# A fused layer-norm kernel: the third row tile loaded alone between Wq and Wk, four roots on ScalarE, and the first transposes in two PSUM banks

## The chip, the cores and the metric

The kernel runs on one core of one Trainium2 chip. The metric is the device time of one execution in microseconds; the span in a profile (first to last instruction) is some 1.7 us shorter than the time of the same run. In the text PE is TensorE, DVE is VectorE, ACT is ScalarE, POOL is GpSimd and SPq is the queue of loads that SyncE issues; PSUM is the memory that PE's results land in, and Wq, Wk and Wv are the thirds of Wqkv.

## The reference, cut to what matters

```python
xn = _layernorm(x)                                  # x: 1 x 2048 x 512, bfloat16
return x + _A_ref(xn, A_wqkv, A_wo) + _B_ref(xn, B_w_gate, B_w_up, B_w_down)
# _A_ref: q, k, v = xn @ wqkv; 32 heads; each row attends to 8 rows, two apart; then @ wo
# _B_ref: (gelu(xn @ w_gate) * (xn @ w_up)) @ w_down
```

Nothing can be multiplied before the first 128 rows of x are loaded, normalised and transposed.

## The kernel before

The kernel is a graph of tasks. A list scheduler in the file orders them by simulated times and priorities when the kernel is built; on the chip each engine runs its list in order and waits on semaphores (in r6 below a copy whose data were there at 7.6 us runs at 9.39, behind the root ahead of it). x is cut into 16 row tiles of 128 rows, four tiles to a block. The first block is handled tile by tile: statistics, mean and root, subtraction, reciprocal, scaling, four transposes on PE, a copy out of PSUM on ACT, then the Q and K projections of that tile.

```python
for i, nm in enumerate(("q", "k", "v")):            # loads of Wqkv, by columns
    ...
    t_w = G.task("sp", "ld_w" + nm, 0, mk(), wr=[(I_wq, nm)],
                 prio=(-958, -957.5, -898)[i], nbytes=512 * 1024)
# ...
if p == 0:                                          # tiles 0 and 1: two loads, ahead of Wq
    ...
else:                                               # tiles 2 and 3: one load, behind Wk (prio -957)
    t_x = G.task("sp", "ld_x%d" % p, 0, mk_ld(), wr=[(it_x, 0), (it_x, 1)], prio=..., nbytes=256 * 1024)
# ...
if t < NSQA:                                        # NSQA = 2: the roots of tiles 0 and 1
    t_of["sq%d" % t] = G.task("act", "sq%d" % t, 0.15, mk_sa(), ..., table="sqrt")
else:                                               # other tiles: add eps on DVE, power 0.5 on GpSimd
    t_of["ve%d" % t] = G.task("dve", "ve%d" % t, 0.09, mk_ve(), ...)
# ...
chain(["bnst0", "bnag0", "sub0", "rstd0", "norm0", "bnst1", "bnag1", "sub1", "rstd1", "norm1",
       "bnst2", "bnag2", "ve2", "sub2", "bnst3", "rstd2", "norm2", "bnag3", "ve3", "sub3", "rstd3",
       "norm3", "bnst4"])                           # DVE's order
# ...
chain(warm_tasks[:WARM[0]] + ["tpx0_0"] + warm_tasks[WARM[0]:] +
      ["mmt0_0", "tpx0_1", "mmt1_0", "mmt0_1", "tpx1_0", "mmt1_1", "tpx1_1",
       "mmt0_2", "mmt1_2", "mmt0_3", "mmt1_3"])     # PE's order; mmt0_t is Q of tile t, mmt1_t is K
```

`SHIFT` is a table of priority offsets by group of tasks, found by search. It decides the order of everything that follows the start.

## Time and profile before

| | before |
|---|---|
| time, median of three runs | 197.85 us (197.62 to 197.93) |
| span of the profiled run | 196.0 us |
| PE busy | 190.6 us, 97% |
| transposes of tile 3 start | 12.15 us |
| last matmul ends | 193.55 us |

The views are read in the prediction below. From the transposes of tile 3 on, PE works without a pause to its last matmul. I call the time from the start of these transposes to that end "the train"; before, it is 193.55-12.15 = 181.40 us. Behind it lies a tail of 2.4 us, the last addition and store.

### The profile page before, as it was taken

Reading aid. Unit: us, or ns where it says so; the run is one execution under the profiler, and the core shown is the slowest. Engines: PE = TensorE matmul, PEld = TensorE weight load, DVE = VectorE, ACT = ScalarE, POOL = GpSimd, SP = SyncE. Lnnn points to the kernel's source line nnn. Section 1 sums busy time; section 2 is a strip of 40 time slices with the busy share of each in tenths; the row PEclk is TensorE's granted clock in tenths of the full one; section 3 lists DMA queues with packets and bytes.
Section 4 is the critical chain, followed back from the end, with each engine's and each line's share of the span. In section 5 each row is a group of like instructions: output and inputs, shape, how many; then the busy total and the mean of one; then the engine's idle time right before and its main releaser. Section 6 shows DMA issues by size and latency. Waiting matters only on the chain.

```text
span 196.0 us, 3243 instructions
## 1 busy us (share of the span) xinstructions
PE 190.6 (97%) x1223; PEld 91.1 (46%) x1223; DVE 153.8 (79%) x241; ACT 104.0 (53%) x169; POOL 9.6 (5%) x33
## 2 busy tenths in 40 slices
PE   7879999999999999999999999999999999999995
PEld 2675444444444344444444444443444444344484
DVE  5689997999699899989989984999966638962232
ACT  3467674777976649502647801667739500776000
POOL 6021000101000000000001100000000000000000
PEclk9999999999999999999999999999999999999999
DMA  5999998949934452262399346003892250020121
GB/s 137 364 410 274 331 201 138 270 116 229 213 72 108 107 151 68 64 168 93 107 204 222 61 113 183 27 0 110 211 229 43 57 160 29 27 59 0 33 87 40
DMA packets 34783, 27.03 MB, mean 138 GB/s; under 512 B 11248, under 2 KB 33232, under 8 KB 34768
## 3 DMA queue, kind: packets, MB, share of 16 engines
q1 hardware_dynamic: 34768, 26.83, 54.0%
q8 instruction: 9, 0.15, 0.3%
q14 instruction: 6, 0.05, 0.1%
HBM read 19.99 MB, written 5.26 MB: 129 GB/s over the span
## 4 chain that ended last, share of the span: by engine, by line
PE 93%; DMA 3%; DVE 2%; SPq 1%; issue 0%; POOL 0%; DVEq 0%
PE PS L1357 36%; PE PS L1436 19%; PE PS L1120 18%; PE PS L1432 7%; PE PS L1326 4%; PE PS L1204 4%; DMA XIN<-in_A_x_dram 3%; PE PS L1076 2%; PE PS L1392 2%; PE PS L1197 1%; DVE st L945 1%; SPq L881 0%; SPq L929 0%; DVE XIN L1001 0%; POOL sq L969 0%
## 5 line engine op out<-in xcount | busy, mean ns | idle before, releaser
L1436 PE MATMUL PS<-Wd,HT 128*128 128x512 bf16 (+2 forms) x209 | 41.3, 345 | 0.0
L1357 PE MATMUL PS<-xnT,Wu 128*128 128x512 bf16 x160 | 40.6, 379 | 0.0
L1357 PE MATMUL PS<-xnT,Wg 128*128 128x512 bf16 x160 | 40.3, 379 | 0.0
L1367 ACT ACTIVATE GG<-PS 128x512 bf16<-128x512 f32 x40 | 23.7, 601 | 28.9 <-PE PS L1357 27.7
L1305 DVE TENSOR_TENSOR UNI<-BS,PT 128x2048 bf16<-128x2048 bf16 x32 | 37.1, 1217 | 2.2 <-PE PS L1326 0.8
L1174 DVE TENSOR_TENSOR UNI<-QT,KT 128x2048 bf16<-128x2048 bf16 x32 | 37.4, 1217 | 0.3 <-PE PS L1326 0.3
L1120 PE MATMUL PS<-xnT,Wqkv 128*128 128x512 bf16 x160 | 36.0, 379 | 0.0
L1374 ACT ACTIVATE UU<-PS 128x512 bf16<-128x512 f32 x40 | 24.0, 600 | 10.5 <-PE PS L1357 10.4
L1436 PEld LDWEIGHTS PS<-Wd,HT 128*128 128x128 bf16 x209 | 19.6, 98 | 18.6
L1456 DVE TENSOR_TENSOR OB<-PS,XR 128x512 bf16<-128x512 f32 (+2 forms) x19 | 11.5, 605 | 17.7 <-PE PS L1436 17.7
L1357 PEld LDWEIGHTS PS<-xnT,Wg 128*128 128x128 bf16 x160 | 15.2, 98 | 19.8 <-issue 0.8
L1357 PEld LDWEIGHTS PS<-xnT,Wu 128*128 128x128 bf16 x160 | 15.4, 98 | 19.4 <-ACT GG L1367 0.8
L1120 PEld LDWEIGHTS PS<-xnT,Wqkv 128*128 128x128 bf16 x160 | 15.4, 98 | 19.2 <-ACT KT L1137 0.4
L1379 DVE TENSOR_TENSOR HT<-GG,UU 128x512 bf16<-128x512 bf16 x40 | 16.1, 420 | 8.8 <-ACT UU L1374 8.4
L1144 ACT ACTIVATE VT<-PS 128x512 bf16<-128x512 f32 x16 | 9.6, 598 | 14.4 <-PE PS L1120 14.4
L1432 PE MATMUL PS<-Wo,OT 128*128 128x512 bf16 (+2 forms) x76 | 16.9, 345 | 0.0
L945 DVE BATCH_NORM_STATS2 st<-XIN 128x6 f32<-128x512 bf16 x16 | 10.6, 684 | 2.0 <-DMA XIN<-in_A_x_dram 2.0
L1337 ACT ACTIVATE OT<-PS 128x512 bf16<-128x512 f32 x16 | 8.7, 594 | 5.4 <-PE PS L1326 5.4
L1432 PEld LDWEIGHTS PS<-Wo,OT 128*128 128x128 bf16 x76 | 7.2, 98 | 7.0
L1137 ACT ACTIVATE KT<-PS 128x512 bf16<-128x512 f32 x12 | 7.2, 597 | 4.8 <-PE PS L1120 4.8
L1130 ACT ACTIVATE QT<-PS 128x512 bf16<-128x512 f32 x12 | 7.2, 598 | 3.8 <-PE PS L1120 3.8
L969 POOL TENSOR_TENSOR sq<-ve,mhalf 128x2 bf16<-128x2 f32 (+1 forms) x8 | 5.5, 686 | 64.3 <-DVE ve L956 64.3
(62 smaller groups left out, 134.1 us busy)
## 6 DMA issues: line engine op xcount, KB each, us to landing
BS<-vt_scratch SPq DMA_DIRECT2D x64, 128.5 KB, 3.5
vt_scratch<-VT SPq DMA_DIRECT2D x16, 128.0 KB
XR<-in_A_x_dram SPq DMA_DIRECT2D x16, 128.0 KB, 2.1
XIN<-in_A_x_dram SPq DMA_DIRECT2D x7, 256.0 KB, 5.9
out_dram<-OB SPq DMA_DIRECT2D x14, 128.0 KB, 2.0
Wqkv<-in_A_wqkv_dram SPq DMA_DIRECT2D x3, 512.0 KB, 4.3
Wg<-in_B_w_gate_dram SPq DMA_DIRECT2D x1, 1280.0 KB
Wu<-in_B_w_up_dram SPq DMA_DIRECT2D x1, 1280.0 KB
```

What stands on the lines that cost most here:

```text
L945: return lambda e: e.bn_stats(out=st[:, t, :], in_=XIN[:, it.slot, t2, :])
L1120: ins = e.matmul(PS[:, 512 * it.slot:512 * it.slot + HWD], lhsT=lhsT, rhs=xnT[:, itx.slot, kt, c0:c0 + HWD], start=(kt == 0), stop=(kt == 3))
L1144: return lambda e: e.activation(out=VT[:, ito.slot, 0:HWD], in_=PS[:, 512 * it.slot:512 * it.slot + HWD], func=ACTF.Identity)
L1174: return lambda e: e.tensor_tensor(out=UNI[:, it.slot, :, :], in0=bass.AP(QT, (itq.slot * 4 + g) * 512, [[NQT * 4 * 512, 128], [0, 4], [1, ...
L1305: return lambda e: e.tensor_tensor(out=bass.AP(UNI, ito.slot * 2048, [[NUNI * 2048, 128], [512, 4], [128, 4], [1, 128]]), in0=bass.AP(BS, ...
L1357: ins = e.matmul(PS[0:M, 512 * it.slot:512 * it.slot + 512], lhsT=Wx[:, kt, j * 128:j * 128 + M], rhs=xnT[:, itx.slot, kt, :], start=(kt = ...
L1367: return lambda e: e.activation(out=GG[0:M, ito.slot, :], in_=PS[0:M, 512 * it.slot:512 * it.slot + 512], func=ACTF.Gelu_apprx_tanh)
L1374: return lambda e: e.activation(out=UU[0:M, ito.slot, :], in_=PS[0:M, 512 * it.slot:512 * it.slot + 512], func=ACTF.Identity)
L1379: return lambda e: e.tensor_tensor(out=HT[0:M, ito.slot, j, :], in0=GG[0:M, ig.slot, :], in1=UU[0:M, iu.slot, :], op=ALU.mult)
L1432: ins = e.matmul(PS[:, 512 * it.slot:512 * it.slot + CW], lhsT=OT[:, ito.slot, dq, ti * 128:(ti + 1) * 128], rhs=Wo[:, dq, c0:c1], start=( ...
L1436: ins = e.matmul(PS[:, 512 * it.slot:512 * it.slot + CW], lhsT=HT[:, ith.slot, j, ti * 128:(ti + 1) * 128], rhs=Wd[:, j, c0:c1], start=Fal ...
L1456: return lambda e: e.tensor_tensor(out=OB[:, ito.slot, 0:CW], in0=PS[:, 512 * it.slot:512 * it.slot + CW], in1=XR[:, itx.slot, c0:c1], op= ...
```

## The change

Its intent: have tile 2 on the chip before DVE is free for it, shorten DVE's work on tiles 2 and 3, and begin the first projection sooner. All priority shifts were searched anew as well.

```diff
 SHIFT = {
-    "acc0": 47, "acc1": -436, "acc3": 127, ...
+    "acc0": 361, "acc1": -284, "acc3": -893, ...        # every value is new
-    NSQA = cfg.get("NSQA", 2)
+    NSQA = cfg.get("NSQA", 4)                            # roots of tiles 0 to 3 on ScalarE
-        WARM = cfg.get("WARM", (9, 1))                   # 9 + 1 warm-up matmuls of 512 columns
+        WARM = cfg.get("WARM", ([512] * 8 + [128], [512, 128]))
...
-            if p == 0:
+            if p < 2:                                    # four loads of one tile each
                 for t2 in range(2):
...
-                    t_x = G.task("sp", "ld_x0_%d" % t2, 0, mk_ld(), wr=[(it_x, t2)], prio=-960 + t2,
+                    t_x = G.task("sp", "ld_x%d_%d" % (p, t2), 0, mk_ld(), wr=[(it_x, t2)],
+                                 prio=((-960, -959), (-957.8, -956.5))[p][t2], nbytes=128 * 1024)
...
+                it_t2 = Item("tpy" + nm, P_ps, "tp") if nm == "0_0" else it_tp      # a second bank
-                                c0 = 1024 * it.slot + kt * 128 * n + q * 128
+                                c0 = 1024 * (it, it2)[kt // 2].slot + kt * 128 * n + q * 128
...
+                if p == 0 and grp[0] == 0:               # DVE copies half of tile 0 out
+                    t_of["evy" + nm] = G.task("dve", "evy" + nm, d_dve(256), mk_ev2(), rd=[it_t2], ...)
...
+        chain(["bnst0", "bnag0", "sub0", "rstd0", "norm0", "bnst1", "bnag1", "evy0_0", "sub1", "rstd1", "norm1",
+               "bnst2", "bnag2", "sub2", "rstd2", "norm2", "bnst3", "bnag3", "sub3", "rstd3", "norm3", "bnst4"])
+                chain(["evk0_0", "sq3"])
```

The queue's order becomes tile 0, tile 1, Wq, tile 2, Wk, tile 3, Wv. Dead code (two tiny touch loads that were never issued) goes as well.

## The prediction

Some passages are cut: figures and rules that no trace or run shows. In the numbered list the second item speaks of ACT and the last of PE's matmuls. The sum came to 197.85-1.35 = 196.5 and, with 0.1 taken off the gain, 196.6. One step loses its ground, the time of ACT's half of the first copy, on which tile 1's root at 6.25 rests. An estimate from the trace of before can stand for it: one column on ACT takes 0.20 us (L850) and 512 take 0.60 (L1037), so 256 take some 0.40, from 5.54 to 5.94, and the root behind them 0.29 (L959), to 6.23. The first projection at 6.1 stands on DVE's half (5.92 to 6.05), which is the later one. "The gate opens" means here that the step between matmuls of 128 columns falls, from 0.107 us in the first transposes to 0.056 in the first projection.

> **What bounds the kernel now.** I read the page first (busy shares, then the slices), then the chain that ended last, then the timeline of the first 16 us, then the waits of the DMA queue. The page says that TensorE is the bound:
>
> ```profile
> PE 190.6 (97%) x1223; PEld 91.1 (46%) x1223; DVE 153.8 (79%) x241; ACT 104.0 (53%) x169; POOL 9.6 (5%) x33
> ...
> PE   7879999999999999999999999999999999999995
> ```
>
> The only slices of PE below nine tenths are the first four and the last one. The chain (start us, length us, what) says what those first slices wait for:
>
> ```profile
> 2.74 5.37 DMA XIN<-in_A_x_dram
> ...
> 8.13 0.70 DVE st L945
> ...
> 10.19 0.35 DVE XIN L1001
> ...
> 10.90 0.61 POOL sq L969
> ...
> 11.74 0.36 DVE XIN L1001
> ...
> 12.15 0.40 PE PS L1026 x4
> 12.55 3.57 PE PS L1076 x64
> ```
>
> After 12.15 every piece of the chain is PE and each begins where the last one ended, up to 193.56; then the last addition and store take the span to 196.0. So the end is 12.15 plus a fixed train of matmuls plus the tail. What moves the time is when that train can begin. Before 12.15 the chain is the third and fourth row tiles: one load that lands at 8.11, the statistics of tile 2 and tile 3 on DVE, and tile 3's root on POOL. The PE timeline shows the hole:
>
> ```profile
> 5.06 0.63 PE L1026 MATMUL PS<-ident,XIN 128*128 128x128 bf16 x4
> 5.49 0.63 PE L864 MATMUL PS<-wsrc 128*128 128x512 bf16 x1
> 6.39 1.07 PE L1076 MATMUL PS<-xnT,Wqkv 128*128 128x128 bf16 x16 [0.26 <-ACT xnT L1037]
> 7.29 0.39 PE L1026 MATMUL PS<-ident,XIN 128*128 128x128 bf16 x4
> 7.51 1.95 PE L1076 MATMUL PS<-xnT,Wqkv 128*128 128x128 bf16 x32
> 10.61 0.40 PE L1026 MATMUL PS<-ident,XIN 128*128 128x128 bf16 x4 [1.14 <-DVE XIN L1001]
> ```
>
> L1026 is a tile's transposes, L1076 its Q or K projection (16 matmuls, 0.90 us apart start to start: 7.29-6.39), L864 the warm-up. PE has nothing real between 9.46 and 10.61, because tile 2 isn't normalised. Two smaller things: the ninth warm-up matmul holds the first transposes to 5.06 though their weight load began at 4.84, and the copy-out of 0.60 us (5.73, ACT L1037) delays the first projection to 6.39. The queue's own waits give the arrival of Wk:
>
> ```profile
> SPq L890 <- DMA Wqkv<-in_A_wqkv_dram: 1.5, 1, 1.5
> ```
>
> L890 loads Wg and is made to wait for Wk; it issues at 7.46, so Wk had landed at 7.44. The projection that needs Wk starts at 7.51: Wk is just in time today.
>
> [...]
> 1. [...]adding up the GB/s slices of the first 12 us, the two first tiles (262 KB) are through near 3.0 us, Wq (786 KB) near 5.2, Wk (1311 KB) near 6.6, the 256 KB load (1573 KB) near 7.3; Wk is known to have landed at 7.44 and the load at 8.11, both some 0.8 us later than their last bytes. [...]
> 2. [...]0.60 us for 512 columns [...], 0.29 to 0.30 for the root with its eps pointer; one table load at 0.79, the next at 19.36, so two more roots near 8 and 10 us cause none.
> [...]
> 4. [...]the warm-ups are 0.43 apart, the first transposes 0.11, the first projection 0.056. So the gate opened between 5.5 and 6.4 us.
>
> **The change part by part.**
> *Warm-up, first copy.* Eight warm-ups and one of 128 columns end at 1.25 + 8 x 0.427 + 0.107 = 4.77 instead of 5.09, so the transposes go when norm 0 allows, near 4.87 (5.06 before): -0.19. Their data is there at 5.69-0.19 = 5.50. [...] DVE copies the other 256, but must first end its aggregate (5.60): from 5.63. This trace's f32 read of 256 PSUM columns on DVE takes 0.42 and of 128 takes 0.29, so I estimate 0.29 to 0.42: ends 5.92 to 6.05. Projection 0 starts near 6.1 instead of 6.39: -0.3.
> *Tile 1.* The DVE copy delays its subtraction from 5.64 to about 6.0, ending 6.35 to 6.4. But the root on ACT, which follows the copy there, comes at 6.25 instead of 6.52. So reciprocal 6.42 to 6.58, scaling to about 6.95 (7.10 before). A wash, slightly early.
> *Tile 2's load.* It moves ahead of Wk: 786 + 131 = 917 KB, whose bytes are through near 5.55; plus the lag of 0.8 it lands near 6.4, against 8.11. DVE is only free at 6.95, so the DMA wait of 1.04 us before L945 goes, and DVE decides. Wk's price is 131 KB at 0.38 KB/ns, 0.35 us: it lands near 7.8. Tile 3's half ends the same bytes as before: about 8.1.
> *Tiles 2 and 3 on DVE.* Before, tile 2 took from 8.13 to 10.54, 2.41 us, with the ve step (0.15), POOL (0.61) and tile 3's statistics in its way. With its root on ACT, tile 0 took from 2.94 to 4.79: 1.85 us. So tile 2: 7.0 to 8.85 (its root on ACT at 7.9 to 8.3, behind the copy of tile 1, which costs me 0.1). Tile 3: 8.95 to 10.8, against 12.09.
> *PE.* Projection q0 6.1 to 7.0, transposes of tile 1 7.03 to 7.25, then a new wait for Wk to 7.8; k0 to 8.7, q1 to 9.6, transposes of tile 2 (ready since 8.9) to 9.82, k1 to 10.72, transposes of tile 3 at about 10.8. Both chains, DVE's and PE's behind Wk, meet within 0.1 us. The unbroken train starts at 10.8 instead of 12.15: -1.35.
> *After that.* Wv follows at 2097 KB, about 9.6, and is wanted at 15.96-1.35 = 14.6; Wg, which waits for Wk, is late by 0.35 at most, and its bytes are through near 13.5, wanted at 18.55-1.35 = 17.2. Neither binds. The matmul work and the last stores are the same; the new shifts only reorder it, and there is no idle PE left there to win.
> Sum: 197.85 - 1.35 = 196.5. I take 0.1 off the gain for small losses in the reordered train: 196.6.
>
> **The rivals.**
> *Wk becomes the wait and eats it.* For: it is just in time today and goes behind 131 KB, and its order on PE is fixed. Against: PE loses at 7.25 to 7.8, where it had over a microsecond of hole later. If Wk came at 8.3, the train would start at 11.3: 197.0.
> *ACT's queue.* ACT gets two roots but also evictions of 0.60 us each, in order. If an eviction of q or k goes ahead of the root of tile 2 or of tile 3, each costs up to 0.6 on DVE's chain: train at 11.3 to 11.5, 197.0 to 197.2. For: ACT is nearly full from 7.7 to 9.3 in the timeline. Against: the roots have the higher priority, and tile 3's is explicitly placed behind k0's eviction, as if this had been looked at.
> *The reordered train has holes.* All shifts are new, so a wait of some tenths for DVE, which is 79% busy and nearly full from 12 to 47 us, or for a PSUM bank may appear: 196.8 to 197.9. Against: the earlier order has none, and everything upstream comes earlier.
> *A cold clock.* If the gate opens as late as 6.4 while q0 starts at 6.1, 0.15 us is lost, all of it inside the wait for Wk: nothing.
>
> **Range and chances.** PE idles only 196.0-190.6 = 5.4 us in all, of which 1.25 is the start before any operand exists and 2.4 the tail. Faster by 2% would be 3.96 us, which needs the train at 8.2, before tile 3 has even been normalised in any version: 1%. Slower by 2% needs 5.3 us of new holes: 1%. Within 2%: 98%. The range: a gain of 1.85 if the DVE chain runs without a hitch and Wk comes early (196.0), a gain of 0.55 if ACT or a hole takes its share (197.3).
>
> **What would show it.** Right: the load of tile 2 lands before 7 us and L945 no longer waits for a DMA there; no POOL root before 12 us; transposes of tile 3 near 10.8; a PE wait of about half a microsecond for Wk, Wg's issue near 7.8; PE without idle time from there to the end; projection q0 near 6.1. Wrong: tile 3's transposes after 11.5 (then ACT's order or Wk), or PE idle time after 12 us (then the shifts), or a tail other than 2.4 us.

## The result and the profile after

| | before | after |
|---|---|---|
| time, median of four runs each | 197.88 us (197.62 to 197.93) | 196.30 us (196.18 to 196.46) |
| ratio | | 0.9923 (95%: 0.9906 to 0.9940) |
| span of the profiled run | 196.0 us | 194.6 us |
| transposes of tile 3 start | 12.15 us | 10.74 us |
| train | 181.40 us | 181.38 us |
| tail | 2.41 us | 2.45 us |

A ratio here is the mean time of one kernel's runs over that of the other's of the same rounds, so it isn't quite the ratio of the medians. The change is 0.8% faster: within 2%, as predicted, at 196.3 where 196.6 was forecast.

The PE timeline of the changed kernel, to be held against the one in the prediction (L1019 is now the transposes, L1077 the projections, L863 the warm-up; columns are start us, length us, engine, line, operation, count):

```profile
4.86 0.61 PE L1019 MATMUL PS<-ident,XIN 128*128 128x128 bf16 x4
5.26 0.67 PE L863 MATMUL PS<-wsrc 128*128 128x512 bf16 x2
6.04 1.05 PE L1077 MATMUL PS<-xnT,Wqkv 128*128 128x128 bf16 x16
6.93 0.39 PE L1019 MATMUL PS<-ident,XIN 128*128 128x128 bf16 x4
7.83 1.96 PE L1077 MATMUL PS<-xnT,Wqkv 128*128 128x128 bf16 x32 [0.51 <-DMA Wqkv<-in_A_wqkv_dram]
9.62 0.39 PE L1019 MATMUL PS<-ident,XIN 128*128 128x128 bf16 x4
9.85 1.06 PE L1077 MATMUL PS<-xnT,Wqkv 128*128 128x128 bf16 x16
10.74 0.39 PE L1019 MATMUL PS<-ident,XIN 128*128 128x128 bf16 x4
10.96 3.74 PE L1077 MATMUL PS<-xnT,Wqkv 128*128 128x128 bf16 x64
```

The hole of 1.14 us before tile 2's transposes is gone. A new and smaller one stands at 7.32 to 7.83, and its releaser is the load of Wk. From 7.83 on PE has no pause: each row shown starts at or before the modelled end of the one above.

DVE of the changed kernel in the same stretch (L937 statistics, L993 scaling, L1031 the new copy):

```profile
5.53 0.26 DVE L1031 COPY xnT<-PS 128x256 bf16<-128x256 bf16 x1
...
6.30 0.35 DVE L993 TENSOR_SCALAR XIN<-XIN,rstd 128x512 bf16<-128x512 bf16 x1
6.57 0.69 DVE L937 BATCH_NORM_STATS2 st<-XIN 128x6 f32<-128x512 bf16 x1
...
8.04 0.35 DVE L993 TENSOR_SCALAR XIN<-XIN,rstd 128x512 bf16<-128x512 bf16 x1
8.31 0.69 DVE L937 BATCH_NORM_STATS2 st<-XIN 128x6 f32<-128x512 bf16 x1
...
9.95 0.35 DVE L993 TENSOR_SCALAR XIN<-XIN,rstd 128x512 bf16<-128x512 bf16 x1
```

Tile 2's statistics follow tile 1's scaling at once, with no wait for a load. Tile 3 is scaled at 10.30, and PE takes it up only at 10.74: DVE has 0.44 us in hand. What holds the start now is PE behind Wk. The semaphore records of the trace hold 16 completions for each load; the last of them came for tile 2 at 6.29, Wk at 7.78, tile 3 at 8.12.

One warning about this trace. The chain of the work that ended last leaves PE between 47 and 72 us and runs over ACT and DVE. The first part of the page (engine, busy us, share of the span, instructions) counts fewer matmuls than weight loads,

```profile
PE 188.5 (97%) x1205; PEld 91.1 (47%) x1224; DVE 153.6 (79%) x240; ACT 104.1 (53%) x171; POOL 8.5 (4%) x31
```

and its PE timeline shows groups such as this one:

```profile
32.80 0.81 PE L1360 MATMUL PS<-xnT,Wu 128*128 128x512 bf16 x3 [0.16 <-issue]
```

That is no new wait. 1224-1205 = 19 matmul records are missing; a group of four such matmuls appears as three with a "gap" of 0.16 us in front. The proof is the train: 181.38 us, as before.

### The profile page after: what moved, and what is told of

Its sections match the earlier page's. It is cut to its first block, busy times and chain, and to the rows that moved or that the text cites. A ratio compares the mean times of both kernels' runs of the same rounds, so it can differ in the third digit from the quotient of the medians.

```text
span 194.6 us, 3228 instructions
## 1 busy us (share of the span) xinstructions
PE 188.5 (97%) x1205; PEld 91.1 (47%) x1224; DVE 153.6 (79%) x240; ACT 104.1 (53%) x171; POOL 8.5 (4%) x31
## 4 chain that ended last, share of the span: by engine, by line
PE 81%; DVE 8%; issue 3%; ACT 3%; DMA 3%; SPq 1%; DVEq 0%; ACTq 0%
PE PS L1360 29%; PE PS L1439 19%; PE PS L1123 13%; PE PS L1435 7%; DVE UNI L1308 4%; PE PS L1329 3%; PE PS L1077 3%; PE PS L1207 3%; DMA Wqkv<-in_A_wqkv_dram 3%; PE PS L1395 1%; DVE UNI L1177 1%; ACT UU L1377 1%; PE PS L1200 1%; DVE HT L1382 1%; DVE HT L1410 1%
## 5 line engine op out<-in xcount | busy, mean ns | idle before, releaser
L1439 PE MATMUL PS<-Wd,HT 128*128 128x512 bf16 (+2 forms) x205 | 40.8, 345 | 0.2
L1360 PE MATMUL PS<-xnT,Wu 128*128 128x512 bf16 x154 | 39.6, 379 | 0.6 <-issue 0.5
L1360 PE MATMUL PS<-xnT,Wg 128*128 128x512 bf16 x156 | 39.4, 379 | 0.4 <-issue 0.3
L1123 PE MATMUL PS<-xnT,Wqkv 128*128 128x512 bf16 x155 | 34.8, 379 | 0.5 <-DVE PS L1245 0.2
L1459 DVE TENSOR_TENSOR OB<-PS,XR 128x512 bf16<-128x512 f32 (+2 forms) x19 | 11.5, 605 | 18.3 <-PE PS L1439 18.3
L937 DVE BATCH_NORM_STATS2 st<-XIN 128x6 f32<-128x512 bf16 x16 | 10.4, 682 | 1.2 <-DMA XIN<-in_A_x_dram 1.2
L1077 PE MATMUL PS<-xnT,Wqkv 128*128 128x128 bf16 x128 | 7.8, 219 | 0.6 <-DMA Wqkv<-in_A_wqkv_dram 0.5
```

The costliest lines, as they stand in the source:

```text
L937: return lambda e: e.bn_stats(out=st[:, t, :], in_=XIN[:, it.slot, t2, :])
L1077: ins = e.matmul(PS[:, 512 * it.slot + 128 * g:512 * it.slot + 128 * g + 128], lhsT=Wqkv[:, kt, which * 512 + g * 128:which * 512 + (g + 1 ...
L1123: ins = e.matmul(PS[:, 512 * it.slot:512 * it.slot + HWD], lhsT=lhsT, rhs=xnT[:, itx.slot, kt, c0:c0 + HWD], start=(kt == 0), stop=(kt == 3))
L1360: ins = e.matmul(PS[0:M, 512 * it.slot:512 * it.slot + 512], lhsT=Wx[:, kt, j * 128:j * 128 + M], rhs=xnT[:, itx.slot, kt, :], start=(kt = ...
L1439: ins = e.matmul(PS[:, 512 * it.slot:512 * it.slot + CW], lhsT=HT[:, ith.slot, j, ti * 128:(ti + 1) * 128], rhs=Wd[:, j, c0:c1], start=Fal ...
L1459: return lambda e: e.tensor_tensor(out=OB[:, ito.slot, 0:CW], in0=PS[:, 512 * it.slot:512 * it.slot + CW], in1=XR[:, itx.slot, c0:c1], op= ...
```

## The experiments

The **head theory**: the time is the start of the train plus a constant (181.4 + 2.45 + 1.75 = 185.6 us), and the train starts when the later of two chains is through, PE behind Wk or DVE's normalisation of tiles 2 and 3. **Rivals**: the roots on ScalarE (or the split copy) bring the gain and the loads do not; the three parts add up evenly; the new order of the later work brings part of it. All kernels gave correct results. Each was timed against the kernel before on the same chip; "start" below is the start of tile 3's transposes in the profiled run.

| run | what it is | start | train | median us | ratio to before |
|---|---|---|---|---|---|
| a0_again | the changed kernel again | 10.80 | 181.39 | 196.38 | 0.9926 |
| r6_loads_undone | changed, loads as before | 12.04 | 181.38 | 197.87 | 1.0001 |
| r5_load_only | before, loads alone changed | 11.09 | 181.40 | 196.59 | 0.9940 |
| r4_two_parts | loads and roots, old shifts | 10.81 | 181.39 | 196.38 | 0.9925 |
| r3_pool_roots | loads and split copy, old shifts | 10.76 | 181.62 | 196.79 | 0.9949 |
| r8_old_shifts | changed, old shifts | 10.64 | 181.61 | 196.55 | 0.9945 |
| r1_wk_last, r1b | changed, Wk behind tile 3 | 12.27, 14.65 | 181.39 | 197.66, 197.46 | 1.0004, 1.0012 |
| r2_wk_first, r2b | changed, Wk ahead of tile 2 | 12.36, 11.80 | 181.39 | 197.45, 197.36 | 0.9980, 0.9979 |
| r10_wk_halves | Wk in two halves, old shifts | 10.62 | 181.50 | 196.58 | 0.9944 |
| r11_x01_act | tile 1's load from ACT's queue | 12.04 | 181.39 | 196.82 | 0.9941 |

Fourteen profiles were taken: before, after and these twelve. In eleven of them the train is 181.38 to 181.40 us. The exceptions are r8 (181.61), r3 (181.62) and r10 (181.50), the three in which the old shifts meet the split copy (see Old shifts). The 95% intervals are 0.1 to 0.7% wide to each side, so ratios of 0.993 and 0.994 aren't told apart by the times; the profiles tell them apart.

### Loads undone, loads alone

The changed kernel with the one load of tiles 2 and 3 behind Wk; the compute engines keep their order.

```diff
-            if p < 2:
+            if p == 0:
...
-                             prio=(0, 0, -897.5, -897)[p] if p < 4 else ...
+                             prio=(0, -957, -897.5, -897)[p] if p < 4 else ...
```

> The changed kernel with the loads of the kernel before (one load for tiles 2 and 3, behind Wk); all compute engines in the same order as in the changed kernel. Head theory: tile 2 lands at 8.11 as before, DVE's chain of 3.7 us ends near 11.85, train at about 11.9, time near 197.5: only about 0.3 of the gain is left. Rival (roots and split copy carry it): 196.8 or less.

Measured: 197.87 us, ratio 1.0001 (0.9972 to 1.0031); the gain is gone. DVE waits for the load again:

```profile
8.24 0.69 DVE L936 BATCH_NORM_STATS2 st<-XIN 128x6 f32<-128x512 bf16 x1 [1.57 <-DMA XIN<-in_A_x_dram]
```

DVE scaled tile 3 at 11.80, near the 11.85 expected, yet PE began its transposes only at 12.04. The reason is ACT's order: tile 2's root stands ahead of tile 1's copy-out, so the copy, whose data were there at 7.6, ran at 9.39 behind a root that waited for the load, and PE came late to the projection that needs it:

```profile
10.02 1.07 PE L1076 MATMUL PS<-xnT,Wqkv 128*128 128x128 bf16 x16 [1.45 <-ACT xnT L1038]
```

So the roots on ScalarE are not free: they can block the queue behind them. With the early load nothing shows of it. Part of what this run loses, 12.04 against the 11.9 expected, belongs to this block and not to the load alone.

The mirror image, the kernel before with the loads alone changed (its edit is the load part of the diff above):

> The kernel before with the loads alone changed. Head theory: DVE starts tile 2 at 7.05, when tile 1 is scaled, and needs 3.96 us with GpSimd's roots: tile 3 scaled at 11.0, PE behind Wk at 10.75, train near 11.05, time 196.7. So the loads alone give 1.1 of the 1.4 us, and DVE, not Wk, sets the start. Rival (the three parts add up, each about a third): 197.4.

Measured: start 11.09 (11.05 expected), 196.59 us, ratio 0.9940 (0.9925 to 0.9955). The loads alone bring the start 12.15-11.09 = 1.06 us forward, of 1.41 in all. DVE sets it here, with GpSimd's roots in its chain, though narrowly: Wk was complete at 7.99 in this run, and PE behind it would have been there at 10.95 (an estimate: 7.99 plus the 2.96 us that PE takes from Wk to there, see the two swaps below).

```profile
10.48 0.16 DVE L978 RECIPROCAL rstd<-sq 128x1 f32<-128x1 bf16 x1 [0.46 <-POOL sq L970]
10.68 0.35 DVE L1002 TENSOR_SCALAR XIN<-XIN,rstd 128x512 bf16<-128x512 bf16 x1
```

The rival of three equal parts (197.4) falls.

### Without the split copy, without the roots

Loads and roots, but one bank, one copy on ACT, nine warm-ups ahead of the transposes, and the shifts of before (the edit, cut):

```diff
-        WARM = cfg.get("WARM", ([512] * 8 + [128], [512, 128]))
+        WARM = cfg.get("WARM", ([512] * 9, [512]))
-                it_t2 = Item("tpy" + nm, P_ps, "tp") if nm == "0_0" else it_tp
+                it_t2 = Item("tpy" + nm, P_ps, "tp") if False else it_tp
-                if p == 0 and grp[0] == 0:
+                if False:
```

> The kernel before with two of the three parts: the loads and the roots on ScalarE, but one bank and one copy for the first transposes, nine warm-ups ahead and one behind, and the old shifts. Head theory: first projection at 6.4 as before, tile 1 scaled at 7.1, tile 2 from 7.1 with its chain of 3.7 us to 10.85, PE behind Wk (7.8) at 10.74: train at 10.9, time 196.5; so the split copy is worth 0.15 us at most. Rival (the split copy and the shorter warm-up are what starts the train earlier): 0.4 us or more lost, 196.9.

Measured: 196.38 us, ratio 0.9925 (0.9900 to 0.9950), start 10.81; the changed kernel on the same chip: 196.38, 0.9926, 10.80. The first projection started at 6.38 instead of 6.04, and it did not matter, since PE met Wk's wait at 7.5 to 7.8 anyway. In this kernel the split copy, the shorter warm-up and the new shifts together are worth nothing that these runs can show.

Loads and split copy, the roots of tiles 2 and 3 back on GpSimd, the shifts of before (the edit, cut):

```diff
-    NSQA = cfg.get("NSQA", 4)
+    NSQA = cfg.get("NSQA", 2)
-               "bnst2", "bnag2", "sub2", "rstd2", "norm2", "bnst3", "bnag3", "sub3", "rstd3", "norm3", "bnst4"])
+               "bnst2", "bnag2", "ve2", "sub2", "bnst3", "rstd2", "norm2", "bnag3", "ve3", "sub3", "rstd3",
+               "norm3", "bnst4"])
-                chain(["evk0_0", "sq3"])
```

> The loads and the split copy, but the roots of tiles 2 and 3 on GpSimd as before (with the DVE order of before for these tiles), old shifts. Head theory: DVE starts tile 2 at 6.5, its chain with GpSimd roots took 3.96 us before (8.13 to 12.09), so tile 3 is scaled near 10.5, still earlier than PE, which is held by Wk until about 10.7: train at 10.7 to 10.8, time 196.3 to 196.5; the roots are worth nothing here. Rival (the roots carry a good part of the gain): train after 11.2, 196.9 or more.

Measured: start 10.76, but 196.79 us, ratio 0.9949 (0.9934 to 0.9964). The start is as expected, though not for the reason given: DVE scaled tile 3 at 10.70, later than the 10.5 expected, and PE, which would have been there at 10.6 (an estimate: Wg's issue, which waits for Wk, came at 7.64, and from Wk on PE takes 2.96), waited 0.1 to 0.2 us for it. The time is worse than the start says, because the train is 181.62 us: 0.23 longer. The next run explains that part. So split copy and roots are two remedies against the same delay on DVE; with either of them, the early load gives nearly all.

### Old shifts

```diff
 SHIFT = {
-    "acc0": 361, ...
+    "acc0": 47, ...                # the whole table of the kernel before
```

> The changed kernel with the priority shifts of the kernel before, so that the later train is in an order not tuned for the new start. Head theory: the head is the same, train at 10.74; if the train has no holes the time is 196.3. Rival (part of the gain comes from the reordering): train longer than 181.4 us, time 196.6 or more.

Measured: start 10.64, train 181.61, 196.55 us, ratio 0.9945 (0.9912 to 0.9979). Here the rival has a point: with the changed start and the old shifts the train is 0.22 us longer. It doesn't wait: no PE row of this train starts after the modelled end of what ran before it. It has another order. The small matmuls (UNI,E) come in twelve groups. In the eleven profiles with a train of 181.4, two of the groups follow each other directly, as in a0_again:

```profile
134.15 1.91 PE L1207 MATMUL PS<-UNI,E 128*32 128x512 bf16 x32
135.88 1.04 PE L1329 MATMUL PS<-UNI,E 128*32 128x512 bf16 x16
```

In r8, and in r3, no two do; here two groups of big matmuls stand between:

```profile
95.65 1.91 PE L1207 MATMUL PS<-UNI,E 128*32 128x512 bf16 x32
97.49 1.04 PE L1360 MATMUL PS<-xnT,Wg 128*128 128x512 bf16 x4
98.37 1.03 PE L1360 MATMUL PS<-xnT,Wu 128*128 128x512 bf16 x4
99.32 1.05 PE L1329 MATMUL PS<-UNI,E 128*32 128x512 bf16 x16
```

From start to start, the step from a big matmul into such a group takes 309 ns and the step out of it 312, against 216 between two big ones and 205 from group to group. One more way in and out costs 309+312-216-205 = 200 ns, nearly all of the 220. The newly searched shifts only save this again; they bring nothing beyond the 181.4 that the kernel before had as well. (r10 keeps its pair of groups; its 0.11 us more are one step of 424 ns instead of 309, at 169.7 us.)

The runs with the head of before's first projection (r4, r5) keep 181.4 with the old shifts.

### Does Wk set the start? Two swaps in the queue

Only two entries of SyncE's list change places; every other engine's list is untouched.

```diff
         G.schedule(SCHED)
+        sp_ = G.order["sp"]
+        nm_ = [q.name for q in sp_]
+        ia_, ib_ = nm_.index("ld_wk"), nm_.index("ld_x1_1")     # r2: "ld_x1_0", "ld_wk"
+        sp_[ia_], sp_[ib_] = sp_[ib_], sp_[ia_]
+        sp_[ia_].start, sp_[ib_].start = sp_[ib_].start, sp_[ia_].start
```

> The changed kernel with one swap in the queue of loads: the second half of tile pair 1 goes ahead of Wk, everything else in the same order. Head theory (the train of matmuls starts when PE, held by Wk, reaches the transposes of tile 3): Wk lands 131 KB later, at 8.1 to 8.2 instead of 7.8, the wait of PE for Wk grows from 0.51 to about 0.85, the transposes of tile 3 move from 10.74 to about 11.08, time 196.6 to 196.7. Rival (the DVE chain with its roots sets the start, the wait for Wk is slack): train at 10.74 still, 196.3.

Measured: 197.66 us, ratio 1.0004 (0.9962 to 1.0046). The direction is right, the size is wrong by 1 us. Wk didn't come 0.35 later but 1.5:

```profile
6.84 0.39 PE L1019 MATMUL PS<-ident,XIN 128*128 128x128 bf16 x4
9.36 1.96 PE L1077 MATMUL PS<-xnT,Wqkv 128*128 128x128 bf16 x32 [2.13 <-DMA Wqkv<-in_A_wqkv_dram]
...
12.27 0.39 PE L1019 MATMUL PS<-ident,XIN 128*128 128x128 bf16 x4
```

PE's answer is that of the head theory. From Wk's last completion to tile 3's transposes it takes 12.27-9.31 = 2.96 us here, 10.74-7.78 = 2.96 in the changed kernel, 10.80-7.84 = 2.96 in its repetition and 10.64-7.68 = 2.96 with the old shifts. So in these runs Wk sets the start, one for one, over a range of 1.6 us. The rival (slack) falls. What failed was my estimate of Wk's arrival, which took the queue for a pipe of 0.38 KB/ns. Eleven of Wk's 16 completions came between 7.20 and 7.78, and five between 8.45 and 9.31. To see whether that was an accident, I ran it again, beside the changed kernel itself:

> The changed kernel itself, unaltered, as a yardstick on this chip. All theories: 196.2 to 196.6, all but the last of the sixteen completions of Wk close together, Wk complete near 7.8, train at 10.6 to 10.8.

> The swap of Wk and the second half of the pair once more (the first time Wk's eighth of sixteen completions came at 7.62 but the last at 9.31, and the time was 197.66 where 196.65 was expected). If the late completion was an accident of that chip or run: Wk complete near 8.15, train near 11.1, 196.6 to 196.7. If the order of the loads itself makes one of the 16 engines late: Wk complete after 9 us again and 197.5 or more.

Measured: the changed kernel 196.38, Wk's completions between 7.10 and 7.84. The swap again 197.46 us, ratio 1.0012 (0.9944 to 1.0080): Wk from 7.72 to 10.06, two completions after 9.8. So it belongs to this order of loads and isn't an accident; the times say so too, since all eight runs of this order took 197.29 us or more where 196.65 was expected. Why a few of the 16 completions come late when both tiles go between Wq and Wk, the records don't say; they bear no number of the DMA engine, so that one engine is late, as the expectation puts it, is not shown. It stays open. The profiled execution of r1b was the slowest of its four (200.20 us) for another reason as well: PE stood idle for 2.67 us, and what followed ran slow:

```profile
10.11 2.89 PE L1077 MATMUL PS<-xnT,Wqkv 128*128 128x128 bf16 x32 [2.67 <-DMA Wqkv<-in_A_wqkv_dram]
```

Thirty-two matmuls took 2.89 us instead of 1.96. In this stretch the trace shows a granted clock of one half (columns: stretch, its us, busy us and count of PE, PEld, DVE, ACT and POOL, granted clock, DMA share, GB/s):

```profile
11.00:12.00 1.00, 1.00 (x13) 1.00 (x11) 0.00 (x0) 0.67 (x2) 0.00 (x0) 0.50 0.82 124
```

Its clock records give the half clock from 10.92 to 14.33 us: it began 0.81 us after PE had resumed. From Wk to tile 3's transposes it took 14.65-10.06 = 4.59 us here instead of 2.96. The wait of 2.13 us in r1 had no such drop behind it. Whether the longer pause brought it on in r1b is not shown: one execution is all there is.

The other swap, Wk ahead of tile 2:

> The changed kernel with the third tile's load put back behind Wk (still split in two). Head theory: Wk at about 7.45, PE doesn't wait for it; tile 2 lands near 7.75 instead of before 6.57, DVE waits for it, and its chain of 3.7 us from tile 2's statistics to tile 3's scaling ends near 11.5; train at about 11.5, time near 197.1. Rival (the roots on ScalarE brought the gain, the place of the load did not): 196.3 or a little less, since PE no longer waits for Wk.

> The third tile's load behind Wk once more (the first time Wq was complete at 6.44, Wk at 8.18, tile 2 at 8.53[...]). Accident: tile 2 complete near 7.8, train near 11.5, 197.1. Made by the order: tile 2 after 8.3 again, train after 12, 197.5 or more.

Measured: 197.45 and 197.36 us, ratios 0.9980 (0.9954 to 1.0005) and 0.9979 (0.9954 to 1.0003). In the first profile (the slowest of its runs, 197.91) Wq, Wk and the tiles were all complete late, each because a few of its 16 completions lagged, tile 2 at 8.53; in the second there was nothing of this, tile 2 at 7.98, and the start was 11.80 where 11.5 was expected. The lists explain most of the 0.3: PE's second Q projection waited for the same blocked copy on ACT as in r6 (1.04 and 1.07 us). So the place of tile 2's load is worth about 1 us, and Wk's own wait, which this swap takes away, can't buy it back.

### Two tries at a faster version

Wk's wait is now the bound, with 0.44 us of slack on DVE behind it. First try, with the old shifts: Wk in two halves of 256 columns, so that the K projection of tile 0 can begin on the first.

```diff
-        for i, nm in enumerate(("q", "k", "v")):
+        for nm, c0, c1, pw in (("q", 0, 512, -958), ("k0", 512, 768, -957.5), ("k", 768, 1024, -957.4),
+                               ("v", 1024, 1536, -898)):
...
+                        if which == 1 and t == 0:            # two tasks of 8 matmuls
+                            for h, nmw in ((0, "k0"), (1, "k")):
```

> The changed kernel (old shifts) with Wk loaded in two halves of 256 columns and the first K projection split into two tasks, so that PE begins it with the first half. Head theory: first half complete near 7.1, second near 7.8; PE no longer idles 0.5 us, reaches tile 3 near 10.3, where DVE has just scaled it (10.2 to 10.35): train near 10.4, time 196.0 to 196.2, faster than the changed kernel by 0.2 to 0.35. Rival (rows of 512 B cost the queue as much time each as rows of 1 KB): Wk's first half at 7.8, the second after 9, train near 11.7, time 197.3.

Measured: 196.58 us, ratio 0.9944 (0.9928 to 0.9961), start 10.62. The halves were complete at 7.30 and 8.11, later than hoped: a row of 512 B took 27 ns in the median, one of 1 KB 46, so two halves cost 54 ns where a whole row costs 46. PE still waited for the second half:

```profile
7.39 0.61 PE L1076 MATMUL PS<-xnT,Wqkv 128*128 128x128 bf16 x8
8.16 1.51 PE L1076 MATMUL PS<-xnT,Wqkv 128*128 128x128 bf16 x24 [0.16 <-DMA Wqkv<-in_A_wqkv_dram]
```

The start is 0.12 earlier than in the changed kernel, but the fair yardstick is r8, which has the old shifts too: start 10.64, 196.55 us. The halves bring 0.02 us of start. PE does half a projection (0.45 us) early, and the second half comes 0.43 later than the whole of Wk in r8 (8.11 against 7.68). Neither the hoped 0.2 to 0.35 nor the rival's loss.

Second try: tile 1's load issued by ACT, so that Wq and everything behind it is issued 0.45 us earlier (Wq at 1.26 instead of 1.71).

```diff
                     t_x = G.task("sp", "ld_x%d_%d" % (p, t2), 0, mk_ld(), ...)
+                    t_x.on_act = (p, t2) == (0, 1)
```

> The changed kernel with the second tile's load issued by ScalarE's queue, beside the first tile's on SyncE's, so that Wq and all behind it are issued 0.46 us earlier; everything else in the same order. Head theory, if Wq's slow start (40 to 170 GB/s between 3.0 and 3.9 us) is a matter of its issue: Wk complete near 7.4 instead of 7.8, PE idles 0.3 instead of 0.7 us, train near 10.4 to 10.5, time 195.9 to 196.1 (0.9905 to 0.9915 of the kernel before). If the slow start belongs to the first rows of the weights and not to the issue, or the two queues slow each other: Wk at 7.7 or later, first tile later than 2.92, train at 10.7 or later, 0.9925 of the kernel before or more.

Measured: 196.82 us, ratio 0.9941 (0.9927 to 0.9954). Wk did come earlier, at 7.10, and the slow stretch before Wq's flow was gone: from 2.4 to 8.1 us no slice of 0.3 us moved less than 300 GB/s, where the changed kernel's slices from 3.0 to 3.9 moved 89, 58 and 167. But tile 0 was complete at 3.77 instead of 2.90: the packets of tile 1, on ACT's queue, started at 1.83, and those of tile 0, on SyncE's, only at 2.37 (1.82 in the changed kernel). DVE began 0.87 later, and the first projection started at 6.76 instead of 6.04. In the profiled run, the slowest of five (197.62), PE also ran it slow, 0.106 us from matmul to matmul instead of 0.056; this trace's clock records begin the full clock only at 9.41 us, those of the ten other profiles that have a record of it between 4.09 and 6.62:

```profile
5.68 0.61 PE L1020 MATMUL PS<-ident,XIN 128*128 128x128 bf16 x4 [0.73 <-DVE XIN L994]
6.08 0.74 PE L863 MATMUL PS<-wsrc 128*128 128x512 bf16 x2
6.76 1.89 PE L1078 MATMUL PS<-xnT,Wqkv 128*128 128x128 bf16 x16
```

At full speed PE's own work from 6.76 on (4.02 us: 0.89 and 0.22 for the first projection and the transposes, 2.91 from there to tile 3's transposes) would end at 10.8, an estimate from the changed kernel's trace: no earlier than there, though Wk came 0.68 sooner. The fastest of the five runs, 196.37, is what this start gives.

So neither version beats the changed kernel.

## Why the prediction was right, point by point

*The bound and the constant train.* Right: the start moved by 1.41 us (1.35 predicted), the train kept its length within 0.02 us, the tail within 0.04.

*The loads.* Right: tile 2 complete at 6.29 (6.4 predicted), Wk 7.78 (7.8), tile 3 8.12 (8.1), Wv 9.69 (9.6). The method, bytes ahead in the queue plus a lag of 0.8 us, was luckier than it looked: r1 shows an order in which it fails by more than 1 us. It was an estimate from the one trace of before. In the thirteen profiles with all early loads in SyncE's queue, the last completions of these loads came in the order of the queue; but the 16 completions of one load of Wk lay 0.4 to 1.2 us apart (7.05 to 7.78 in the changed kernel), with both tiles between Wq and Wk even from 7.20 to 9.31 and from 7.72 to 10.06, and PE took Wk up only behind the last (7.83 in the changed kernel, 9.36 in r1).

*Warm-up and first copy.* Right in its own times (transposes 4.86, first projection 6.04, 4.87 and 6.1 predicted), without effect on the result, as r4 shows. The DVE copy was over-estimated: 0.26 us, not 0.29 to 0.42, since I scaled it from reads of f32 (0.29 us for 128 columns, 0.42 for 256); this copy reads 256 columns of bf16. ACT's half took 0.38 us.

*Tile 1, "a wash".* Off: tile 1 was scaled at 6.65, 0.45 us earlier than before where I said 0.15. The copy was shorter and began inside the tail of the aggregate (5.53, the aggregate runs from 5.43 to 5.61), and the root on ACT came at 5.78 to 6.07 instead of ending at 6.25.

*"Both chains meet within 0.1 us."* Wrong: DVE is through at 10.30 and PE at 10.74. DVE's 3.73 us from tile 2's statistics to tile 3's scaling were right, but they began at 6.57 instead of 7.0. The start was unharmed, because Wk decides.

*The order on ACT.* I put tile 2's root behind tile 1's copy; it is ahead of it. In the changed kernel the copy ran at 7.71 instead of about 7.4, hidden by the wait for Wk; in r6 and r2 the same order cost PE over 1 us of waiting (1.45 and 1.04).

*The discount of 0.1 us for losses in the reordered train.* Not needed, though not baseless: with the old shifts r8's train is 0.22 us longer, by one more change between kinds of matmul and not by the waits that the prediction had in mind; the new shifts avoid it.

*The rest of the difference.* Predicted gain 1.25, measured 1.58 in the medians. The start gives 1.41. I set the profiled run of before (197.67 us) beside the median of 197.85; that run was 0.2 us faster than the median. 197.67-1.41 = 196.26, which is the measured time. That the profiled run was a fast one could have been seen. Whether the slower runs of before lose their 0.2 us in the start wasn't profiled.

*The rivals.* Wk did become the wait, as the first of them said, at the predicted 7.8 and no later. ACT's queue and a cold clock did not show in the changed kernel; both showed in experiments (r6 and r2; r11 and r1b). The full clock of the kernel before began at 6.26 us by its clock records, inside the predicted 5.5 to 6.4.

*A slip in reading.* The prediction counts four slices of PE below nine tenths at the start; the line has three (7, 8, 7). The start of the train at 12.15 lies in the third, so nothing rests on it.

## What to carry to other kernels

When one engine runs without a pause to the end, measure the length of that train (here 181.38 to 181.40 us in eleven of fourteen profiles) and look only at what starts it: every change of the head then has an exact price, and a part whose effect ends in another wait (here the split copy) is seen to be worth nothing. In a start-up, the order of the loads was the strongest lever, about 1 us of 1.4 for moving 128 KB by one place; check each new order by the last completion of each load, not by its bytes. Where an engine runs its list in order, as ACT does here, a small new task whose input comes late blocks everything behind it (1.45 us of PE's time in r6), so ask what stands next in that queue.
